# Gated linear attention and an MLP on one core: 32x32 transposes of alpha, k and q done in place, the reordering left to the readers

## The chip, the cores and the metric

The kernel runs on one core of a Trainium2 chip. The time is device microseconds of one execution; lower is better. Five engines each take their own instructions in the order in which the program issued them: TensorE (PE, with its weight loads shown apart as PEld), VectorE (DVE), ScalarE (ACT), GpSimd (POOL) and SyncE (SP, which here issues the DMAs).

## The reference

```python
# q, k, v, alpha: (4, 8, 768, 48) float32;  alpha in [0.8, 1)
state = np.zeros((B, H, D, D))
for t in range(S):
    state = alpha[:, :, t, :, None] * state + np.einsum('bhd,bhe->bhde', k[:, :, t], v[:, :, t])
    y[:, :, t] = np.einsum('bhd,bhde->bhe', q[:, :, t], state)

x = y.transpose(0, 2, 1, 3).reshape(3072, 384)     # tokens x (heads*dim)
h = x @ w_in                                        # 384 x 2048
g = h * np.clip(h + 3.0, 0.0, 6.0) / 6.0            # hardswish
out = g @ w_out                                     # 2048 x 384
```

## The kernel before

**Chunks.** The 4 x 768 tokens are cut into 24 chunks of 128 (six to a batch entry). A chunk j turns the recurrence into matrix products: with running products of alpha along the tokens, k is scaled by a decay and q by a growth, `scores` multiplies the two, `masked` cuts the upper triangle, `attend` multiplies with v and with the state of the chunk before, and `update`/`next_state` carry the state on. All this wants alpha, k and q with heads and dims on the partitions and tokens in the free direction, in four tiles of 128 x 128 (two heads each), while the inputs have tokens first.

**How the inputs are turned.** Chunks 0 to 5 are turned by TensorE through PSUM. From chunk 6 on (`FIRST`) each of alpha, k and q is loaded into a "quad" tile `quads[name, j % 2]` of 128 x (4, 4, 48), whose 32-partition groups and 32-column pieces are 32x32 blocks, and `by_blocks` (line 286) has VectorE transpose the blocks. A load spreads neighbouring tokens over the blocks: token 4u+v of a tile lies in block v at column u. So `by_blocks` writes each transposed block with a step of four elements into the tile where tokens stand in order: `aX` for alpha (step `ca`), `Ks` for k (`tk`), `Qs` for q (`tq`).

**The steps of a chunk around the change.** `la`, `lk`, `lq` load into the quads; `ca.j` places alpha; `decay` (`r.j`, line 309) is a scan over alpha on VectorE and `growth` (`p.j`, line 320) another; `scaled` multiplies k by the decay (`k.j`) and q by the growth (`q.j`), both at line 332, in place in `Ks` and `Qs`. From chunk 8 on `turn_k` (`kt.j`, line 391) transposes the scaled k by blocks back into the k quad, from which two DMAs (`kw`, `kr`) make the copy with tokens on the partitions. ScalarE's steps are copies and activations: `qa` (line 366) and `sv` (line 419) place q and the state for `attend` (`ya`, `yb`, line 455), `cy` (line 464) keeps the chunk's y.

**The MLP.** Two chunks make a group g. Both products use sums of blocks that save multiplications (combined weights and combined x and g, made by VectorE). `M.g.i` (line 600) are the 20 products of the first layer. ScalarE copies some of them out of PSUM (`n.g.i`, line 606), VectorE adds them (`o`, lines 537 to 541), ScalarE applies the Relu part of hardswish (`e`, line 494) and VectorE the rest (`h`, line 498). VectorE makes sums of g (`s`, lines 647 and 664), `P.g.i` (line 703) are the seven products of the second layer, ScalarE keeps three of them half-way (`K.g.i`, line 682) and VectorE and ScalarE make the outputs (`G`, lines 719 and 716). The weights come first: float64 bits are loaded and turned to float32 by steps `w` and `d1` to `d4` on ScalarE, VectorE and GpSimd (`d1.i` is line 186, `d4.i` line 217), while the first six chunks run, and `x` (line 647) and `y` (lines 537 to 541) make the combined weights of the second and the first layer.

**The order.** All steps are written out by hand as words in one list (`ca.16` is step `ca` of chunk 16, `K.5.2` step `K` of group 5, number 2). The program issues them in that order, and every engine works off its own instructions in that order; semaphores make an instruction wait for what it needs. For the neighbourhoods that the prediction uses, the list reads:

```
fr.0.4.0 d3.14 k.6 q.6 ca.7 fg.0.4 d1.14 d4.14 x.0 y.1
qa.15.0 ... ca.16 lv.18.2 lk.17 la.18 sv.18.0 K.5.2 e.6.1.1 n.6.18.10 K.5.1 P.5.5 G.5.2.3 r.16 k.16
n.6.13.14 o.6.4.0 ca.17 o.6.2.0 ya.15.1 ya.14.2 yb.14 sv.15.1 yb.15 cy.15
n.9.10.10 ca.22 r.22 k.22 sm.20.1 m.20 st.21 p.21 q.21 qa.20.0
```

Of the kernel before, what the change touches and what calls it, by code (L numbers as in the profile page):

```python
# [13 lines left out]
ALU = mybir.AluOpType  # L14
# [3 lines left out]
def kernel(  # L18
# [32 lines left out]
    nc = tc.nc  # L51
# [9 lines left out]
    G = 2  # L61
    GT = G * C
    HB = C // 2
    W = C + 1
# [169 lines left out]
    BLK = 32  # L234
# [39 lines left out]
    def transposed(name, j, i=None):  # L274
        if j >= FIRST:
            t = (K_t if name == "k" else Q_t)[j] = (Ks if name == "k" else Qs)[j % 2]
            by_blocks(t, name, j)
            return
        t = bank("t" + name, j, i)
        src = ring[name, j % NR]  # L280
        for p in range(NP):
            nc.tensor.transpose(  # L282
                t[:, p], src[:, 2 * p : 2 * p + 2].rearrange("s h d -> s (h d)"), ident)

    def by_blocks(to, name, j):
        nc.vector.transpose(out=to.rearrange("r p (u v) -> r p v u", v=V),
                            in_=quads[name, j % NQ][:, :, :, 0:BLK])
# [6 lines left out]
    def without_first(t):  # L294
        return t[:, 0 : NP * W].rearrange("r (p w) -> r p w", w=W)[:, :, 1:W]

    def place_alpha(j):
        to = without_first(aX[j % 2])
        if j < FIRST:
            nc.scalar.copy(out=to, in_=ps_t.pop(("ta", j)))  # L300
        else:
            by_blocks(to, "a", j)
# [21 lines left out]
    def scaled(name, j):  # L324

        if j < FIRST:
            src = ps_t.pop(("t" + name, j))
            t = (Ks if name == "k" else Qs)[j % 2]
        else:
            src = t = (K_t if name == "k" else Q_t)[j]  # L330
        by = R_t[j][:, :, 1:W] if name == "k" else without_first(P_t.pop(j))
        nc.vector.tensor_tensor(out=t, in0=src, in1=by, op=ALU.mult)  # L332
        (K_t if name == "k" else Q_t)[j] = t
# [416 lines left out]
    with tc.manual_schedule():  # L750
# [3 lines left out]
               dx.0 w.2 d2.2 kb.1.0 ck.1 lq.1 r.2 sm.0.1 st.1 tq.1.2 q.1 d3.2 z.0.3 d1.2 dx.2 lv.1.1  # L754
               u.1.3.1 sv.1.0 sm.1.0 p.2 sm.1.1 sc.1.0.2 m.1 ya.0.3 yb.0 cy.0 lq.2 w.1 d1.1 tq.2.1
               q.2 d4.2 lk.2 tk.2.3 k.2 fa.2.0 d4.0 st.2 sc.2.0.2 d2.1 d3.1 m.2 dx.1 d4.1 qa.1.1
               lk.3 la.3 ta.3.1 ca.3 la.4 fa.0.1 sv.1.1 w.3 r.3 ta.4.3 ca.4 r.4 tk.3.1 k.3 kb.2.0
               qa.1.0 d2.3 ya.1.2 yb.1 cy.1 fa.1.2 lq.3 ck.2 d1.3 p.3 d3.3 lv.2.2 u.2.3.2 sm.2.0
               d4.3 fb.2 tq.3.1 q.3 fb.1 qa.2.0 sm.2.1 sv.2.0 st.3 fr.0.2.0 fg.0.2 lk.4 tk.4.0
               sv.2.1 w.5 d2.5 k.4 d3.5 d1.5 qa.3.0 d4.5 qa.2.1 sc.3.1.3 m.3 w.6 d2.6 d1.6 d3.6 d4.6  # L760
               lv.3.0 lq.4 w.7 kb.3.2 fb.0 f.0.3.3 kb.4.0 ya.2.1 ck.3 u.3.3.2 sm.3.0 fr.0.3.1 fg.0.3
               fr.0.1.0 fg.0.1 qa.3.1 sv.3.0 sm.3.1 p.4 d2.7 sv.3.1 d1.7 d3.7 d4.7 f.0.5.0 fr.0.5.1
               fr.0.0.0 fg.0.5 fg.0.0 tq.4.3 ck.4 la.5 ta.5.2 f.0.6.3 ca.5 w.4 d2.4 ya.3.0 yb.3 cy.3
               fr.0.6.1 yb.2 cy.2 w.9 d2.9 q.4 qa.4.1 d1.4 d1.9 dx.4 la.6 w.8 d3.4 r.5 lk.5 w.10
               d3.9 p.5 ca.6 fg.0.6 d4.9 w.12 lq.5 lv.4.1 d2.8 d3.8 f.0.7.2 d1.8 st.4 d4.8 d4.4 w.11
               fr.0.7.0 fg.0.7 f.1.7.0 fr.1.7.1 fg.1.7 sc.4.0.2 m.4 f.1.1.1 fr.1.1.0 fg.1.1 f.1.3.3
               fr.1.3.1 d2.10 d1.10 tk.5.3 f.1.0.2 d2.12 d3.10 d4.10 w.13 fg.1.3 fr.1.0.0 fg.1.0 k.5
               d3.12 lq.6 f.1.6.0 f.1.2.1 u.4.1.0 sm.4.0 d1.12 d4.12 sv.4.0 qa.4.0 ya.4.2 fr.1.6.1
               fg.1.6 w.15 tq.5.3 fa.4.3 sv.4.1 d2.11 kb.5.1 d2.13 fr.1.2.0 f.1.4.2 fr.1.4.1 d1.11
               sm.4.1 q.5 r.6 d3.11 d3.13 fg.1.4 d4.11 lv.5.0 lk.6 tq.6 p.6 d2.15 d3.15 fg.1.2 d1.13  # L770
               d4.13 sc.5.0.3 yb.4 f.1.5.0 fr.1.5.1 fg.1.5 tk.6 m.5 b.1.0.2 fb.4 b.1.1 d1.15 d4.15
               st.5 y.5 w.14 la.7 lk.7 cy.4 d2.14 qa.5.1 ck.5 b.0.0.1 fr.0.4.0 d3.14 k.6 q.6 ca.7
               fg.0.4 d1.14 d4.14 x.0 y.1 y.10 b.0.1 y.0 y.2 u.5.2 P.1.0.0 K.1.0 qa.5.0 sv.5.0
               qa.6.1 P.1.1.3 b.0.2 b.1.2 kb.6.0 ya.5.3 y.6 s.1.0.0 sm.5.0 sv.5.1 G.1.0.0 tk.7
               s.1.1.1 s.1.2.3 x.1 yb.5 cy.5 b.1.3 sc.6.1.2 lv.6.2 ck.6 u.6.3.0 s.1.3.2 x.2 P.1.2
               b.0.3 K.1.1 y.7 s.1.4 s.1.5 y.11 y.3 r.7 xc.2.1 x.3 y.4 y.8 xc.2.3 k.7 xc.2.0 xc.2.4
               y.9 y.12 y.16 y.13 y.15 P.1.3.3 K.1.2 P.1.4 bo.1 P.1.5 xc.2.5 G.1.1.1 P.1.6 y.14 y.17
               y.19 xc.2.6 sm.6.0 G.1.2.2 y.20 M.2.0.2 lv.12.1 la.8 O.1.1 O.1.0 ca.8 y.18 y.21 y.23
               so.1 G.1.3.3 n.2.0.8 bo.0 lq.7 lv.7.0 O.1.2 m.6 xc.2.2 xc.2.10 xc.2.7 tq.7 r.8 p.7
               xc.2.8 sv.6.1 M.2.15.3 M.2.1 kb.7.3 n.2.1.9 M.2.16 M.2.2 n.2.2.10 M.2.7.0 n.2.7.11  # L780
               sm.6.1 xc.2.9 q.7 p.8 M.2.3 M.2.4 n.2.4.12 M.2.8 o.2.0.0 M.2.5 n.2.5.13 qa.7.0 sv.6.0
               st.7 lk.8 O.1.3 lq.8 lk.9 la.9 la.10 tk.8 tq.8 lq.10 lq.9 ya.6.1 yb.6 M.2.9 z.1.3
               M.2.18.1 o.2.1.0 e.2.1.1 M.2.10 cy.6 ck.7 sc.7.0.2 u.7.1.3 n.2.10.14 M.2.11 qa.7.1
               ca.9 la.11 y.22 M.2.6.2 h.2.1 q.8 m.7 e.2.0.0 h.2.0 n.2.11.15 qa.6.0 n.2.18.10 qa.8.1
               M.2.12 M.2.19 n.2.12.12 M.2.13 sm.7.0 sv.7.1 r.9 k.8 o.2.3.0 sv.7.0 ya.7.0 y.24
               o.2.5.0 n.2.13.12 o.2.2.0 yb.7 cy.7 sc.8.1.2 xc.3.1 o.2.2.1 e.2.2.1 xc.3.3 o.2.3.1
               M.2.14 xc.3.4 xc.3.0 xc.3.5 o.2.4.0 xc.3.7 xc.3.6 o.2.6.0 P.2.0.1 M.3.0.2 M.2.17
               h.2.2 o.2.6.1 e.2.3.0 h.2.3 o.2.7.0 K.2.0 n.3.0.12 M.3.1 n.3.1.9 e.2.5.1 M.3.7.0
               n.3.7.13 xc.3.8 o.2.7.1 xc.3.2 kt.8 e.2.6.0 h.2.6 tk.9 M.3.2 n.3.2.10 e.2.4.0 P.2.1.3
               h.2.4 h.2.5 s.2.0.14 e.2.7.0 G.2.0.1 h.2.7 M.3.3 M.3.4 n.3.4.8 k.9 s.2.1.11 M.3.8  # L790
               o.3.0.0 ca.10 kt.9 P.2.3.3 s.2.2.15 s.2.3.14 lv.8.2 kw.8 kr.8 lk.10 sm.7.1 xc.3.9
               M.3.5 n.3.5.11 K.2.2 e.3.0.1 xc.3.10 M.3.9 o.3.1.0 P.2.2 K.2.1 u.8.0.3 M.3.18.2 s.2.5
               M.3.10 n.3.10.14 n.3.18.15 e.3.1.0 s.2.4 P.2.4 tq.9 h.3.0 st.8 sv.8.0 M.3.11 n.3.11.8
               tk.10 p.9 sm.8.0 q.9 r.10 k.10 qa.9.0 qa.9.1 m.8 sm.8.1 h.3.1 M.3.19 o.3.5.0 kt.10
               P.2.5 G.2.2.0 st.9 M.3.12 sc.9.0.1 qa.8.0 n.3.12.10 o.3.3.0 kw.9 lv.9.0 kr.9 sv.8.1
               u.9.2.3 sm.9.0 sv.9.1 sv.9.0 G.2.1.2 sm.9.1 st.10 M.3.15.2 M.3.16 M.3.6.3 M.3.13 m.9
               o.3.4.0 o.3.6.0 tq.10 n.3.13.10 o.3.2.0 e.3.4.1 ya.8.2 yb.8 ya.9.3 yb.9 cy.9 M.3.14
               M.3.17 cy.8 xc.4.1 P.2.6 e.3.5.0 G.2.3.3 o.3.2.1 xc.4.3 h.3.4 xc.4.4 o.3.6.1 xc.4.5
               xc.4.0 xc.4.6 e.3.2.1 M.4.0.0 n.4.0.10 P.3.0.1 xc.4.7 o.3.7.0 p.10 h.3.5 o.3.3.1
               xc.4.8 M.4.7.3 M.4.1 xc.4.2 h.3.2 o.3.7.1 lk.11 O.2.2 tk.11 e.3.6.0 e.3.3.1 h.3.3  # L800
               P.3.1.2 e.3.7.1 n.4.1.13 M.4.2 K.3.0 ca.11 q.10 h.3.6 r.11 k.11 h.3.7 n.4.7.15
               lv.10.2 lv.11.0 kw.10 sc.10.0.1 kr.10 G.3.0.0 u.10.3.2 sm.10.0 qa.10.1 n.4.2.14 M.4.3
               M.4.4 M.4.8 s.3.0.9 xc.4.9 s.3.2.12 s.3.1.11 P.3.3.2 n.4.4.8 M.4.5 o.4.0.0 e.4.0.0
               sv.10.1 sm.10.1 xc.4.10 kt.11 O.2.0 O.2.3 lq.11 m.10 s.3.3.9 s.3.5 M.4.9 o.4.1.0
               P.3.2 sv.10.0 st.11 n.4.5.11 K.3.2 la.13 M.4.18.0 p.11 tq.11 lk.12 tk.12 K.3.1 M.4.10
               n.4.10.9 q.11 qa.10.0 n.4.18.12 e.4.1.1 la.12 s.3.4 ca.12 h.4.0 r.12 P.3.5 G.3.2.1
               h.4.1 M.4.11 P.3.4 n.4.11.8 M.4.12 n.4.12.14 qa.11.0 M.4.19 p.12 G.3.1.3 lq.12 kw.11
               O.2.1 tq.12 kr.11 u.11.3 sc.11.0.2 sv.11.0 O.3.1 lk.13 P.3.6 qa.11.1 M.4.6.2 G.3.3.2
               k.12 o.4.3.0 m.11 sm.11.0 sv.11.1 kt.12 M.4.13 n.4.13.14 q.12 o.4.3.1 e.4.3.0 o.4.2.0
# [6 lines left out]
               lq.13 O.3.0 O.3.3 lv.13.2 kw.13 O.4.0 lq.14 tq.13 lq.15 M.5.3 M.5.4 M.5.8 s.4.3.10  # L816
# [116 lines left out]
```

## Time and profile before

| what | value |
|---|---|
| median of 3 runs | 535.56 us (535.33 to 535.83) |
| span of the profiled execution, first to last instruction | 533.7 us |
| busy: PE, PEld, DVE, ACT, POOL | 524.6, 499.4, 477.2, 257.2, 50.4 us |
| line 286 transposes (54) | 20.1 + 20.1 + 20.2 us |
| line 332 products of chunks 6 on (36) | 12.2 + 13.6 us |
| granted TensorE clock | 1.000 |

The profile is one execution, and its own time is the span; what lies around the span (about 1.9 us against the median of the timed runs) has no instruction of the program in it. In the views, "line engine operation out<-in xcount | busy, mean ns of one | idle before" is a group of instructions; a timeline row gives the start in us from the beginning of the span, the time taken, and the idle time before it with what ended it. Neighbouring instructions of an engine overlap a little, so that a duration is some tens of nanoseconds more than the distance to the next start. A view does not print the words of the order: they were matched to the rows by counting each engine's instructions in the order of the list.

### The profile page before, as it was taken

Reading aid. Unit: us, or ns where it says so; the run is one execution under the profiler, and the core shown is the slowest. Engines: PE = TensorE matmul, PEld = TensorE weight load, DVE = VectorE, ACT = ScalarE, POOL = GpSimd, SP = SyncE. Lnnn points to the kernel's source line nnn. Section 1 sums busy time; section 2 is a strip of 40 time slices with the busy share of each in tenths; the row PEclk is TensorE's granted clock in tenths of the full one; section 3 lists DMA queues with packets and bytes.
Section 4 is the critical chain, followed back from the end, with each engine's and each line's share of the span. In section 5 each row is a group of like instructions: output and inputs, shape, how many; then the busy total and the mean of one; then the engine's idle time right before and its main releaser. Section 6 shows DMA issues by size and latency. Waiting matters only on the chain.

```text
span 533.7 us, 15143 instructions
## 1 busy us (share of the span) xinstructions
PE 524.6 (98%) x6306; PEld 499.4 (94%) x6306; DVE 477.2 (89%) x849; ACT 257.2 (48%) x503; POOL 50.4 (9%) x71
## 2 busy tenths in 40 slices
PE   8799999999999999999999999999999999999997
PEld 7698886789999999999999999999999999999997
DVE  6999989999999999998999999999999899496382
ACT  3889865212653553553544444642634544553340
POOL 5333425100000000000000000000000000000000
DMA  9998876005615155254344355044454042100001
GB/s 174 217 252 256 215 216 152 21 2 154 152 30 116 32 121 135 57 140 95 87 110 113 91 124 140 19 120 102 115 136 104 11 110 43 44 2 2 15 16 37
DMA packets 124100, 54.40 MB, mean 102 GB/s; under 512 B 83328, under 2 KB 116864, under 8 KB 124032
## 3 DMA queue, kind: packets, MB, share of 16 engines
q1 hardware_dynamic: 124032, 53.44, 42.5%
q8 instruction: 49, 0.80, 0.6%
q14 instruction: 19, 0.16, 0.1%
HBM read 44.50 MB, written 8.91 MB: 100 GB/s over the span
## 4 chain that ended last, share of the span: by engine, by line
PE 85%; DVE 8%; POOL 2%; DMA 2%; ACT 1%; issue 1%; SPq 1%; DVEq 0%; POOLq 0%
PE m_ps L703 34%; PE m_ps L600 34%; PE m_ps L478 5%; PE t_ps L455 4%; PE t_ps L346 2%; PE t_ps L429 2%; PE m_ps L489 2%; PE t_ps L282 1%; DVE rings L647 1%; DMA v<-in_v_dram 1%; DVE raw L537 1%; ACT raw L191 1%; DMA kq<-in_k_dram 1%; DVE g_sb L647 1%; DVE w L537 1%
## 5 line engine op out<-in xcount | busy, mean ns | idle before, releaser
L606 ACT COPY g_sb<-m_ps 128x512 f32<-128x512 f32 x110 | 63.6, 584 | 124.9 <-PE m_ps L600 104.1
L703 PE MATMUL m_ps<-w,g_sb 128*128 128x192 f32 x704 | 121.7, 327 | 0.0
L703 PEld LDWEIGHTS m_ps<-w,g_sb 128*128 128x128 f32 x704 | 113.7, 190 | 0.4
L703 PE MATMUL m_ps<-rings,g_sb 128*128 128x192 f32 x528 | 91.5, 326 | 0.0
L703 PEld LDWEIGHTS m_ps<-rings,g_sb 128*128 128x128 f32 x528 | 85.4, 190 | 0.1
L600 PE MATMUL m_ps<-xc,w 128*128 128x128 f32 x640 | 82.7, 277 | 0.3 <-DVE w L541 0.3
L600 PEld LDWEIGHTS m_ps<-xc,w 128*128 128x128 f32 x640 | 77.5, 192 | 1.5 <-issue 0.5
L494 ACT ACTIVATE r<-g_sb,half 128x512 f32<-128x512 f32 x80 | 56.8, 722 | 32.9 <-DVE g_sb L541 12.1
L498 DVE SCALAR_TENSOR_TENSOR g_sb<-r,g_sb 128x512 f32<-128x512 f32 x80 | 53.6, 682 | 4.6 <-ACT r L494 4.2
L600 PE MATMUL m_ps<-xT,raw 128*128 128x128 f32 x400 | 52.5, 277 | 0.0
L600 PEld LDWEIGHTS m_ps<-xT,raw 128*128 128x128 f32 x400 | 48.6, 192 | 0.6
L409 POOL TENSOR_TENSOR st<-sm,R 128x192 f32<-128x192 f32 x20 | 12.9, 643 | 353.8 <-DVE sm L439 306.7
L647 DVE TENSOR_TENSOR g_sb<-g_sb 128x512 f32<-128x512 f32 (+1 forms) x55 | 42.0, 795 | 0.2
L600 PE MATMUL m_ps<-xT,w 128*128 128x128 f32 x320 | 42.0, 276 | 0.0
L600 PEld LDWEIGHTS m_ps<-xT,w 128*128 128x128 f32 x320 | 39.3, 192 | 0.1
L366 ACT COPY A<-q 48x256 f32<-48x256 f32 x88 | 35.5, 404 | 5.0 <-DVE q L332 3.7
L356 DVE TENSOR_TENSOR A<-t_ps,mask 64x256 f32<-64x256 f32 x96 | 36.0, 414 | 0.4
L478 PE MATMUL m_ps<-xT,w 128*128 128x256 f32 x144 | 32.8, 382 | 0.0
L600 PE MATMUL m_ps<-xc,raw 128*128 128x128 f32 x240 | 31.8, 276 | 0.0
L309 DVE TENSOR_TENSOR_SCAN R<-t,ones 128x516 f32<-128x516 f32 x24 | 29.7, 1236 | 1.1 <-ACT t L300 1.0
L478 PEld LDWEIGHTS m_ps<-xT,w 128*128 128x128 f32 x144 | 26.7, 190 | 3.6
L600 PEld LDWEIGHTS m_ps<-xc,raw 128*128 128x128 f32 x240 | 29.6, 192 | 0.1
(104 smaller groups left out, 731.0 us busy)
## 6 DMA issues: line engine op xcount, KB each, us to landing
raw<-in_moe_w_out_dram SPq DMA_DIRECT2D x8, 768.0 KB, 5.2
raw<-in_moe_w_in_dram SPq DMA_DIRECT2D x6, 768.0 KB, 6.8
v<-in_v_dram SPq DMA_DIRECT2D x48, 96.0 KB, 3.0
out_dram<-oh SPq DMA_DIRECT2D x44, 96.0 KB, 1.7
far<-kq SPq DMA_DIRECT2D x64, 64.0 KB, 2.2
kb<-far SPq DMA_DIRECT2D x64, 64.0 KB, 2.0
aq<-in_alpha_dram SPq DMA_DIRECT2D x36, 96.0 KB, 2.5
qq<-in_q_dram SPq DMA_DIRECT2D x36, 96.0 KB, 2.4
```

The source lines that it names most:

```text
L309: nc.vector.tensor_tensor_scan(out=reverse(R, n - 1, n), data0=reverse(ax, n, n), data1=reverse(ones, n, n), initial=0.0, op0=ALU.mult, op ...
L356: nc.vector.tensor_tensor(out=to[:, a], in0=sc[a][half], in1=mask[half, half].unsqueeze(1).to_broadcast([HB, NP, HB]), op=ALU.mult)
L366: nc.scalar.copy(out=to[:, a], in_=Q_t[j][64 * a : 64 * a + D, :, half])
L409: nc.gpsimd.tensor_tensor(out=st, in0=sm, in1=R_t[j][:, :, 0:1].to_broadcast([C, NP, D]), op=ALU.mult)
L455: nc.tensor.matmul(y_of(j, (i + 1) // 2, p)[:, HB * b : HB * b + HB], vb[:, p, e : e + 32], A_t[j][:, b, 2 * p + a], start=(b == 0 and i = ...
L478: nc.tensor.matmul(h[:, f], w1[:, kk, o : o + C], xT_t[g][:, kk], start=(kk == 0), stop=(kk == KT - 1))
L494: nc.scalar.activation(out=to, in_=h, func=AF.Relu, bias=half, scale=1.0 / 6.0)
L498: nc.vector.scalar_tensor_tensor(out=to, in0=r, scalar=1.0, in1=h, op0=ALU.min, op1=ALU.mult)
L600: nc.tensor.matmul(acc[g][i][:, f * C : (f + 1) * C], spots[w][:, f * C : (f + 1) * C], x_of(g, x), start=(first and f == 0), stop=last, s ...
L606: nc.scalar.copy(out=slots[z], in_=acc[g][i])
L647: nc.vector.tensor_tensor(out=out, in0=in0, in1=in1, op=ALU.subtract)
L703: nc.tensor.matmul(to[g], a, rhs[:, f], start=(first and f == 0), stop=(last and f == HF - 1), skip_group_check=True)
```

## The change

For chunks 6 on, `by_blocks` transposes each block onto itself, with runs of 32 neighbouring elements on both sides. Nothing is reordered there. `scaled` reads its first operand from the quad in permuted order: consecutive elements lie 48 elements (192 bytes) apart, four of them, and then the next token by one element; its second operand and its output are contiguous. For alpha a new instruction on ScalarE (`nc.scalar.copy`, in step `ca.j` right after the transpose) reads the quad in that permuted order and writes `aX` in order. The quad of q is thereby read until `q.j` rather than until `tq.j`, and five loads of q (`lq.10`, `lq.15`, `lq.18`, `lq.21`, `lq.22`) stand later in the list, each behind the `q` step of two chunks before. No other word moves.

```diff
     def transposed(name, j, i=None):
         if j >= FIRST:
-            t = (K_t if name == "k" else Q_t)[j] = (Ks if name == "k" else Qs)[j % 2]
-            by_blocks(t, name, j)
+            by_blocks(name, j)
             return
...
-    def by_blocks(to, name, j):
-        nc.vector.transpose(out=to.rearrange("r p (u v) -> r p v u", v=V),
-                            in_=quads[name, j % NQ][:, :, :, 0:BLK])
+    def blocks(name, j):
+        return quads[name, j % NQ][:, :, :, 0:BLK]
+
+    def by_blocks(name, j):
+        nc.vector.transpose(out=blocks(name, j), in_=blocks(name, j))
+
+    def by_fours(t):
+        return t.rearrange("r p (u v) -> r p u v", v=V)
+
+    def in_order(name, j):
+        return blocks(name, j).rearrange("r p v u -> r p u v")
...
     def place_alpha(j):
...
         else:
-            by_blocks(to, "a", j)
+            by_blocks("a", j)
+            nc.scalar.copy(out=by_fours(to), in_=in_order("a", j))
...
     def scaled(name, j):
+        t = (Ks if name == "k" else Qs)[j % 2]
+        by = R_t[j][:, :, 1:W] if name == "k" else without_first(P_t.pop(j))
         if j < FIRST:
-            src = ps_t.pop(("t" + name, j))
-            t = (Ks if name == "k" else Qs)[j % 2]
+            nc.vector.tensor_tensor(out=t, in0=ps_t.pop(("t" + name, j)), in1=by, op=ALU.mult)
         else:
-            src = t = (K_t if name == "k" else Q_t)[j]
-        by = R_t[j][:, :, 1:W] if name == "k" else without_first(P_t.pop(j))
-        nc.vector.tensor_tensor(out=t, in0=src, in1=by, op=ALU.mult)
+            nc.vector.tensor_tensor(out=by_fours(t), in0=in_order(name, j), in1=by_fours(by),
+                                    op=ALU.mult)
         (K_t if name == "k" else Q_t)[j] = t
```

## The prediction

> **What bounds the kernel now.** I read the page's busy times and slices first, then busy time by stretches, then the groups by shape, then the timeline around each `ca` step.
>
> ```profile
> span 533.7 us, 15143 instructions
> ...
> PE 524.6 (98%) x6306; PEld 499.4 (94%) x6306; DVE 477.2 (89%) x849; ACT 257.2 (48%) x503; POOL 50.4 (9%) x71
> ...
> PE   8799999999999999999999999999999999999997
> ...
> DVE  6999989999999999998999999999999899496382
> ```
>
> ```profile
> 128.00:440.00 312.00, 311.96 (x4042) 306.64 (x4043) 298.67 (x551) 147.71 (x309) 10.63 (x16) 1.00 0.43 100
> ```
>
> From 128 to 440 us PE shows 311.96 of 312 us busy at clock 1.00, and its weight loads 306.64. So PE is the bound; freeing another engine can return at most the 5.4 us in which no weight load ran. DVE is busy 298.67, idle 13.3: it runs right behind PE and often delivers just in time. ACT is half idle. So the change has little to win, and what counts is whom it makes wait.
>
> ```profile
> L286 DVE STREAM_TRANSPOSE t<-aq 128x512 f32<-128x512 f32 x18 | 20.1, 1115 | 0.0
> L332 DVE TENSOR_TENSOR q<-q,P 128x512 f32<-128x512 f32 x18 | 13.6, 754 | 0.1
> L332 DVE TENSOR_TENSOR k<-k,R 128x512 f32<-128x512 f32 x18 | 12.2, 676 | 0.0
> L391 DVE STREAM_TRANSPOSE kq<-k 128x512 f32<-128x512 f32 x16 | 11.2, 697 | 0.0
> L191 ACT ACTIVATE raw<-raw 128x768 f16<-128x768 int32 x3 | 5.8, 1941 | 0.1
> L606 ACT COPY g_sb<-m_ps 128x512 f32<-128x512 f32 x110 | 63.6, 584 | 124.9 <-PE m_ps L600 104.1 <-DVE g_sb L647 9.7 <-DVE g_sb L498 5.7
> ```
>
> **Transposes.** Line 286 writes with a step of 16 bytes, 1.12 us; line 391 has the same size and runs on both sides, 0.70 us. In place all runs are contiguous: 3 x 0.42 = 1.26 us less DVE time per chunk, 18 chunks.
>
> **Products.** No row reads with a large step on DVE. Below, 0.68 us as now; above, twice that, 1.36. If a scattered read costs what the scattered write cost, 0.68 + 0.42 = 1.10. I take 1.2, between the last two: +0.52 for each. DVE per chunk is then -1.26 + 1.04 = -0.22 us, 4 us in all (ends: -22.7 and +1.8 us over the run).
>
> [...]
>
> **The copy on ACT.** 0.58 us as the contiguous copy of line 606; above, line 191's 1941 ns for 768 scattered elements, 1.29 us for 512. I take 0.58 + 0.42 = 1.0. As work, 18 us on a half-idle engine cost nothing. As a place in ACT's queue it costs: the copy cannot start before DVE's transpose, all of ACT's later steps stand behind it, and DVE works later than the list suggests. Hence I went through all 18 places: copy start = the later of the transpose's end less 0.42 and the end of ACT's step before; the following steps shift by what is left; a consumer is late by what exceeds its slack. Chunk 16 is the clearest (ACT, DVE, PE):
>
> ```profile
> 291.49 0.32 ACT L682 COPY p<-m_ps 128x192 f32<-128x192 f32 x1
> 291.84 0.72 ACT L494 ACTIVATE r<-g_sb,half 128x512 f32<-128x512 f32 x1
> ...
> 294.59 1.12 DVE L286 STREAM_TRANSPOSE t<-aq 128x512 f32<-128x512 f32 x1
> 296.50 0.36 DVE L719 TENSOR_TENSOR oh<-m_ps,u 128x192 f32<-128x192 f32 x1 [0.79 <-issue]
> ...
> 293.64 2.77 PE L703 MATMUL m_ps<-w,g_sb 128*128 128x192 f32 x16
> ```
>
> `ca.16` stands ahead of `K.5.2` (the line 682 row) in the list. Now ACT starts `K.5.2` at 291.49, three microseconds before DVE gets to the transpose. After, ACT stands still until then. DVE last waited for PE at 268.9; since then it ran three of the transposes (-1.26) and three products (+1.56): +0.30. Transpose end 295.71 + 0.30 - 0.42 = 295.59, copy to 296.59, `K.5.2` to 296.95 with a hand-over. `P.5.5` (PE, 293.64) writes on into the bank that `K.5.2` copies: **3.3 us** of standing PE. The rest of that queue (`n.6.18.10`, `n.6.10.15`) is late by less.
>
> Chunk 17: `sv.15.1` starts at 306.34, `ca.17`'s transpose ends at 308.46, and `yb.15` on PE already waits for `sv.15.1`. DVE itself slips about 2.2 us behind chunk 16's jam (`G.5.2.3` waits for `K.5.1`, then k.16 +0.52, one transpose -0.42): transpose end 308.46 + 2.2 - 0.42 = 310.2, copy to 311.25, `sv.15.1` to 312.0 where it ended at 307.07: 4.9, of which 3.3 is counted: **1.6 us**.
>
> Chunk 22: `ca.22` and `r.22` are neighbours, and the copy has to follow `n.9.10.10`.
>
> ```profile
> 415.38 0.59 ACT L606 COPY g_sb<-m_ps 128x512 f32<-128x512 f32 x1 [4.22 <-PE m_ps L600]
> ...
> 413.04 1.10 DVE L286 STREAM_TRANSPOSE t<-aq 128x512 f32<-128x512 f32 x1
> 414.17 1.23 DVE L309 TENSOR_TENSOR_SCAN R<-t,ones 128x516 f32<-128x516 f32 x1
> ```
>
> The copy runs 415.97 to 416.97, the scan starts at 417.05 instead of 414.17: 2.9 us of standing DVE, and `k.22`, `sm.20.1`, `m.20` queue behind it. With `k.22`'s +0.52, `m.20` ends 3.4 us later; it ended 0.85 us before `ya.20`: **2.5 us**.
>
> Chunk 9: DVE is early, but ACT is busy to 142.10 and its next copies (`n.2.11`, `n.2.12`) end 0.11 us before PE continues in their banks. 1.0 us of copy plus the 0.2 that the row of steps loses: **1.2 us**. Chunk 19: ACT stands from 338.8 to about 342, `n.7.12.11` reaches `M.7.13` late by 0.5 to 1.1: **0.8**. Chunk 18: `e.6.5.1` 1.2 late, `h.6.5`, `h.6.7` behind it with 0.62 us of slack before `P.6.3`: **0.5**. Chunk 11: `n.4.2.14` 0.82 late against 0.39: **0.4**.
>
> Chunk 7, in the weights stage, where DVE is busy 47.59 of 48 us (80 to 128) and PE waits for its last weight sum (0.29 us at 128.04): the copy now stands ahead of `d1.14` (ACT, 90.15 to 91.08), which `d4.14` (POOL) and then `x.0` (DVE, 96.43) need. Two transposes (-0.84), k.6 (+0.52) and q.6 come before; q.6 took 1.95 because POOL's `d4.14` ran beside it, which moves away: 1.2, -0.75. Transpose end 95.79 - 1.07 - 0.42 = 94.3; copy to 95.35, `d1.14` 0.93, `d4.14` 1.46 (the undisturbed row at 86.03): `x.0` at 97.85, +1.4. Two transposes and one product up to 128: -0.3. **1.1 us**.
>
> Chunks 6, 8, 10, 12 to 15, 20, 21, 23: the delayed steps (up to 2.2 us) have more slack than that on the way to PE; chunk 6's 1.2 us on DVE ends in the 1.28 us wait before `sm.4.0`. If that cover were gone, each would cost PE its 0.5 to 2 us.
>
> **Loads.** The same DMAs in number and size. The five moved `lq` pass `la.11` and a few words of SP's queue and wait for a `q` step; they land about 2.4 us after issue and are wanted tens of microseconds later. `la` now waits for ACT's copy rather than the transpose, by one to two microseconds, ahead of loads wanted later: nothing.
>
> **Sum.** 3.3 + 1.6 + 2.5 + 1.2 + 0.8 + 0.5 + 0.4 + 1.1 = 11.4 us. Against it, a late PE gives DVE a lead, and DVE is 0.22 us a chunk shorter, so part of the 5.4 us of loading gaps closes; I take 1.4. +10.0 us on the span: 543.7; the median lies 1.9 above the span: **545.6 us**.
>
> **Rivals.**
> *Blocks absorbed.* With products at 0.68 and the copy at 0.58, DVE reaches each transpose up to 1.3 us earlier: chunk 16 gives 1.35, 17 1.0, 22 1.6, 9 0.7, 7 nothing, 4.6 together, less up to 3 closed gaps: +1.6 to +4, 537 to 539.5. For it: the contiguous rows; against: line 286's price for scattered access. 0.14.
> *Faster.* The same prices, and each lead of 1.26 us per chunk lasts to the next `ca`, so that ACT never stands: PE gets back half of its 5.4 us: 532.9. It decides only if DVE's waits behind PE (1.19 us at 187, 1.35 at 247) do not eat the lead; they do. 0.08.
> *DVE becomes the bound.* The in-place transposes stay at 1.12 (the 48-element pitch sets it, not the write), so the change does not do what it says, or the reads cost 2 us: +1.0 to +1.4 per chunk, 17 to 25 us on DVE against 13.3 idle, and each jam grows by about 1 us: +17 to +25, 553 to 561. 0.12.
> *No difference.* Delays and recovered gaps cancel. 0.04.
>
> **Numbers.** The forecast (slower by 4 to 17 us) has 0.62. Two tenths of a per cent, 1.07 us, is what a measurement of this kernel can tell. Slower 0.62 + 0.14 + 0.12 = 0.88, same 0.04, faster 0.08. For 8 in 10 the range runs from the absorbed case's lower end, 537, to 556, inside the DVE-bound case.
>
> **What would show it.** Line 286 near 0.70 us; line 332 of chunks 6 on near 1.2 us; a new ACT copy near 1.0 us, waiting for line 286 some 20 us in total; PE waits in front of `P.5.5`, `yb.15`, `ya.20` and near 143 us; DVE waiting for ACT before line 309. Wrong: PE as full as now from 128 to 440, or DVE with no idle time left there.

## The result and the profile after

The changed kernel takes 551.43 us (median of 4 runs, 551.35 to 553.21) against 535.69 before on the same chip: a ratio of 1.0302, 95% interval 1.0287 to 1.0316. It is 15.7 us slower; the forecast was +10, with a range that reaches to 556. The span of the profiled execution grew from 533.7 to 549.6 us, by 15.9. (The run of 553.21 us had a mean granted clock of 0.991, the other three 0.994; what the clock does is shown below.)

The page of the changed kernel, the same rows as before:

```profile
span 549.6 us, 15194 instructions
...
PE 530.2 (96%) x6306; PEld 502.6 (91%) x6306; DVE 469.8 (85%) x849; ACT 274.9 (50%) x521; POOL 50.3 (9%) x71
...
PE   7799999999999999999997899899999899999997
...
DVE  6999898899999899998896878799989799497282
```

VectorE has 7.4 us less work than before (477.2), ScalarE 17.7 us more, and neither is busier than 85%. What is new are the slices of PE that are no longer full, in the second half of the run. The stretch from 128 to 440 us shows the same:

```profile
128.00:440.00 312.00, 302.36 (x3813) 295.13 (x3812) 279.53 (x522) 155.29 (x311) 10.44 (x15) 0.99 0.42 96
```

PE is busy 302.36 us of 312 (311.96 before) and VectorE 279.53 (298.67 before). No engine took over as the bound: both wait more. The clock column says 0.99, where it said 1.00; that is the second loss, shown below.

The groups by shape give the prices (line numbers moved by up to ten; 288 are the transposes, 339 the products, 310 the new copy):

```profile
L310 ACT COPY t<-aq 128x512 f32<-128x512 f32 x18 | 19.4, 1080 | 34.3 <-DVE aq L288 31.6 <-DMA kb<-far 2.7
L339 DVE TENSOR_TENSOR q<-qq,P 128x512 f32<-128x512 f32 x18 | 18.4, 1024 | 0.1
L339 DVE TENSOR_TENSOR k<-kq,R 128x512 f32<-128x512 f32 x18 | 18.3, 1019 | 0.0
L288 DVE STREAM_TRANSPOSE aq<-aq 128x512 f32<-128x512 f32 x18 | 12.6, 699 | 0.1
```

A transpose in place takes 0.70 us (1.12 before), a product 1.02 (0.68), the copy 1.08. The number to look at is behind the bar of the first row: ScalarE stood 34.3 us in front of these 18 copies, 31.6 of it waiting for the transposes of line 288. ScalarE is busy for only 50% of the run, and a wait of it need not cost anything (in a version below these copies wait 17.0 us and the time is that of the kernel before); here the steps behind it were due.

The timeline around chunk 16 (ScalarE, VectorE, TensorE):

```profile
297.29 1.05 ACT L310 COPY t<-aq 128x512 f32<-128x512 f32 x1 [3.86 <-DVE aq L288]
298.25 0.31 ACT L690 COPY p<-m_ps 128x192 f32<-128x192 f32 x1
...
296.54 0.71 DVE L288 STREAM_TRANSPOSE aq<-aq 128x512 f32<-128x512 f32 x1
303.25 0.36 DVE L727 TENSOR_TENSOR oh<-m_ps,u 128x192 f32<-128x192 f32 x1 [6.00 <-issue]
...
298.61 4.55 PE L711 MATMUL m_ps<-w,g_sb 128*128 128x192 f32 x16 [2.76 <-ACT p L690]
```

ScalarE waits 3.86 us for the transpose, copies, and only then makes `K.5.2` (line 690), for which TensorE has stood 2.76 us. And then `P.5.5`, 2.77 us before, takes 4.55. (Its sixteen rows, x16, are eight products: the trace counts each twice.) Two stretches of the windows, one at this place and one at chunk 17, with the granted clock third from the end:

```profile
298.60:303.00 4.40, 4.39 (x17) 4.39 (x18) 0.00 (x0) 3.06 (x7) 0.00 (x0) 0.61 0.74 162
...
316.20:320.30 4.10, 4.10 (x48) 3.82 (x49) 0.98 (x3) 1.21 (x4) 0.00 (x0) 0.58 0.54 118
```

After each of the two longest waits, 2.76 and 2.25 us, the clock falls, to 0.61 and 0.58 on average over these stretches: (1 - 0.61) x 4.4 + (1 - 0.58) x 4.1 = 3.4 us of TensorE's time. The other places, on the timeline, chunks 7, 17, 19 and 22 in order:

```profile
97.77 1.76 DVE L655 TENSOR_TENSOR rings<-w 128x1536 f32<-128x1536 f32 x1 [2.82 <-POOL w L217]
...
316.17 1.03 PE L463 MATMUL t_ps<-A,v 128*32 128x64 f32 x32 [2.25 <-ACT v L427]
...
355.37 0.71 ACT L427 COPY v<-s 48x192 f32<-48x192 f32 x2
355.40 1.16 PE L608 MATMUL m_ps<-xc,raw 128*128 128x128 f32 x8 [0.76 <-ACT g_sb L614]
...
356.17 0.36 DVE L447 TENSOR_TENSOR s<-t_ps,st 128x192 f32<-128x192 f32 x1 [3.13 <-issue]
...
357.78 0.94 PE L608 MATMUL m_ps<-xT,raw 128*128 128x128 f32 x6 [1.23 <-DVE g_sb L545]
...
431.19 1.23 DVE L317 TENSOR_TENSOR_SCAN R<-t,ones 128x516 f32<-128x516 f32 x1 [3.34 <-ACT t L310]
434.28 1.56 PE L463 MATMUL t_ps<-A,v 128*32 128x64 f32 x64 [1.35 <-DVE A L364]
```

The brackets name what a row waited for: `x.0` for the weight step on GpSimd, `yb.15` for ScalarE's `sv.15.1`, `M.7.13` for `n.7.12.11`, `M.7.15` for VectorE, the scan `r.22` for the copy, `ya.20` for the mask behind that scan. The bracket of the row at 356.17 (`sm.17.0`) names nothing; just before it, at 356.08, ScalarE's `sv.16.1` (the row at 355.37) ended.

### The profile page after: what moved, and what is told of

Same layout as the page of the kernel before. It is cut to its first block, busy times and chain, and to the rows that moved or that the text cites. A ratio compares the mean times of both kernels' runs of the same rounds, so it can differ in the third digit from the quotient of the medians.

```text
span 549.6 us, 15194 instructions
## 1 busy us (share of the span) xinstructions
PE 530.2 (96%) x6306; PEld 502.6 (91%) x6306; DVE 469.8 (85%) x849; ACT 274.9 (50%) x521; POOL 50.3 (9%) x71
## 5 line engine op out<-in xcount | busy, mean ns | idle before, releaser
L711 PE MATMUL m_ps<-w,g_sb 128*128 128x192 f32 x704 | 123.8, 330 | 2.8 <-ACT p L690 2.8
L711 PEld LDWEIGHTS m_ps<-w,g_sb 128*128 128x128 f32 x704 | 115.3, 192 | 3.8 <-ACT p L690 2.9
L608 PE MATMUL m_ps<-xc,w 128*128 128x128 f32 x640 | 84.4, 280 | 1.2 <-DVE w L549 0.7
L608 PEld LDWEIGHTS m_ps<-xc,w 128*128 128x128 f32 x640 | 78.8, 194 | 2.7 <-ACT g_sb L614 1.5
L608 PEld LDWEIGHTS m_ps<-xT,w 128*128 128x128 f32 x320 | 39.3, 192 | 0.1
L310 ACT COPY t<-aq 128x512 f32<-128x512 f32 x18 | 19.4, 1080 | 34.3 <-DVE aq L288 31.6
L463 PE MATMUL t_ps<-A,v 128*32 128x64 f32 x1536 | 26.5, 221 | 4.7 <-ACT v L427 2.2
```

The lines of the kernel that those rows point to most:

```text
L310: nc.scalar.copy(out=by_fours(to), in_=in_order("a", j))
L463: nc.tensor.matmul(y_of(j, (i + 1) // 2, p)[:, HB * b : HB * b + HB], vb[:, p, e : e + 32], A_t[j][:, b, 2 * p + a], start=(b == 0 and i = ...
L608: nc.tensor.matmul(acc[g][i][:, f * C : (f + 1) * C], spots[w][:, f * C : (f + 1) * C], x_of(g, x), start=(first and f == 0), stop=last, s ...
L711: nc.tensor.matmul(to[g], a, rhs[:, f], start=(first and f == 0), stop=(last and f == HF - 1), skip_group_check=True)
```

## Experiments

Two theories. **Queue:** the loss comes from the place of the alpha copy in an engine's queue, ahead of steps that are due, and from the clock that falls after the longest waits. **VectorE:** it comes from the products' permuted reads, which make VectorE late. All ratios are against the kernel before, on the same chip. Differences to the changed kernel (551.43 us) are between medians that were not all taken on one chip; the kernel before measured 535.46 to 535.69 us beside them.

**k and q alone.** Alpha goes the old way; no copy on ScalarE.

```diff
-            by_blocks("a", j)
-            nc.scalar.copy(out=by_fours(to), in_=in_order("a", j))
+            nc.vector.transpose(out=to.rearrange("r p (u v) -> r p v u", v=V),
+                                in_=blocks("a", j))
```

> Queue theory (the loss comes from the place of the alpha copy in ScalarE's queue): k and q are turned in place and their products read in permuted order, alpha goes the old way with no copy on ScalarE; VectorE saves 2 x 0.42 and pays 2 x 0.34 us a chunk, so nothing waits anew: 534.5 to 536.5 us, within 0.2% of the kernel before. VectorE theory (the loss comes from the permuted reads of the products): about 551 us, as all of them are in it.

536.06 us, ratio 1.0015 (1.0006 to 1.0025). All 36 permuted products are in it, at 1.02 and 1.09 us, and the whole version is only 0.6 us slower. The VectorE theory falls.

**Alpha alone.** k and q go the old way.

```diff
-            by_blocks(name, j)
+            t = (K_t if name == "k" else Q_t)[j] = (Ks if name == "k" else Qs)[j % 2]
+            nc.vector.transpose(out=t.rearrange("r p (u v) -> r p v u", v=V), in_=blocks(name, j))
...
-            nc.vector.tensor_tensor(out=by_fours(t), in0=in_order(name, j), in1=by_fours(by),
-                                    op=ALU.mult)
+            nc.vector.tensor_tensor(out=t, in0=t, in1=by, op=ALU.mult)
```

> Queue theory: only alpha is turned in place and put in order by ScalarE, k and q as before; all the jams of ScalarE's queue are there: 548 to 553 us, line 310 waiting some 30 us for the transposes. VectorE theory: the products are at 0.68 us again and one transpose a chunk is shorter, so VectorE has 7.5 us less to do than before: 533 to 536 us.

549.65 us, ratio 1.0272 (1.0256 to 1.0287): 14.2 of the 15.7 us with only the copy on ScalarE and one shorter transpose. The run in its profile, whose two longest waits are those of the changed kernel (2.8 and 2.3 us) and whose mean clock is 0.994 as there, took 551.23 us, as long as the changed kernel; the other three, with a mean clock of 0.997, took 549.43 to 549.85. So what is missing goes with the clock and not with the products, as far as four runs tell. The group row of the copy reads as in the changed kernel:

```profile
L311 ACT COPY t<-aq 128x512 f32<-128x512 f32 x18 | 19.4, 1080 | 32.5 <-DVE aq L289 32.4
```

**One place mended, chunk 16.** `ca.16` is split into the transpose `cb.16`, which stays, and the copy `cc.16`, four ScalarE steps later.

```diff
-ca.16 lv.18.2 lk.17 la.18 sv.18.0 K.5.2 e.6.1.1 n.6.18.10 K.5.1 P.5.5
+cb.16 lv.18.2 lk.17 sv.18.0 K.5.2 e.6.1.1 n.6.18.10 K.5.1 cc.16 la.18 P.5.5
```

> The changed kernel, with one word moved: the copy of chunk 16's alpha stands behind K.5.1 in ScalarE's queue instead of ahead of K.5.2 (the next load of alpha into that quad follows it). Queue theory: P.5.5 no longer waits 2.8 us and TensorE's clock does not fall after it (1.8 us); chunk 17's jam stays or grows a little: 545.5 to 548 us. VectorE theory: no VectorE instruction is changed, 551 to 552 us.

547.52 us, ratio 1.0233 (1.0201 to 1.0266): 3.9 us less than the changed kernel. Timeline of that kernel, ScalarE and TensorE:

```profile
293.99 0.32 ACT L696 COPY p<-m_ps 128x192 f32<-128x192 f32 x1
...
297.83 1.07 ACT L316 COPY t<-aq 128x512 f32<-128x512 f32 x1 [1.45 <-DVE aq L288]
...
296.23 2.77 PE L717 MATMUL m_ps<-w,g_sb 128*128 128x192 f32 x16
```

`K.5.2` runs almost four microseconds ahead of the copy, `P.5.5` no longer waits and takes 2.77 us, as in the kernel before at clock 1.00. The jam of chunk 17 is still there: `yb.15` waits 2.1 us.

**Keeping TensorE busy in the two longest waits.** Unneeded products fill them; the waits stay.

```diff
-P.5.5
+zt.1.12 P.5.5        # 12 x matmul(banks[1][:, 0:C], ident, ident)
...
-yb.15
+zt.0.10 yb.15        # 10 of them into banks[0]
```

> The changed kernel with 12 unneeded 128x128 products ahead of P.5.5 and 10 ahead of yb.15, into PSUM banks that are free there; the waits themselves stay. If the clock fell to one half because TensorE stood still: P.5.5's sixteen products take 2.8 us instead of 4.55 and the time is 2.5 to 3.5 us less, 548 to 549 us. If those stretches are slow for another reason (ScalarE's late n.6.18.10, VectorE): 551 to 552 us.

548.48 us, ratio 1.0248 (1.0232 to 1.0264), 2.95 us less than the changed kernel, with more instructions. Its timeline of TensorE, the filling (line 544) first:

```profile
295.62 2.84 PE L544 MATMUL t_ps<-ident 128*128 128x128 f32 x24
298.58 2.87 PE L715 MATMUL m_ps<-w,g_sb 128*128 128x192 f32 x16
```

(The trace counts each product twice, here 12 as x24, as in `P.5.5`.) `P.5.5` starts at 298.58, as late as in the changed kernel (298.61), but takes 2.87 us and not 4.55, and the clock of the run is 1.000. So these 3 us belong to the clock, and they come on top of the waits.

**The copy on GpSimd.**

```diff
-            nc.scalar.copy(out=by_fours(to), in_=in_order("a", j))
+            nc.gpsimd.tensor_copy(out=by_fours(to), in_=in_order("a", j))
```

> The changed kernel with the copy of alpha on GpSimd instead of ScalarE, at the same places in the list. Queue theory: ScalarE's queue is as before and its jams are gone; GpSimd's copy, estimated at 1.5 to 2.5 us, makes the decay scan wait where it follows closely (chunks 11, 12, 16, 22): 536 to 542 us. If any copy between transpose and scan costs the time, whatever engine makes it: 550 us or more. VectorE theory: 551 us.

540.06 us, ratio 1.0087 (1.0072 to 1.0102). The copy takes 1.25 us there; the 1.5 to 2.5 us expected were an estimate that no run shows. About half of what is left, 2.2 us, comes at one place, on the timeline of GpSimd and TensorE:

```profile
267.64 1.06 POOL L310 COPY t<-aq 128x512 f32<-128x512 f32 x1 [12.91 <-DMA v<-in_v_dram]
268.76 0.52 POOL L423 MEMSET v<- 64x512 f32 x1
...
269.34 1.55 PE L463 MATMUL t_ps<-A,v 128*32 128x64 f32 x96 [2.05 <-POOL v L423]
```

Here the copy of chunk 15 stands ahead of GpSimd's memset for `sv.12.0`, which `ya.12` needs: the same jam on another engine. (The bracket of the copy's row names a DMA of long before; its transpose had just ended.) The time is as expected, but not for the reason given: the scans of chunks 11, 12, 16 and 22 made TensorE lose next to nothing; it fell behind at chunks 7 and 15, where other steps of GpSimd stood behind the copy, and by smaller steps elsewhere.

**The same with two words moved:** the copy of chunk 7 behind `d4.14`, that of chunk 15 behind `sv.12.0`.

```diff
-ca.7 fg.0.4 d1.14 d4.14 x.0
+cb.7 fg.0.4 d1.14 d4.14 cc.7 x.0
...
-ca.15 sv.12.0
+cb.15 sv.12.0 cc.15
```

> The kernel with the copy on GpSimd, with two words moved: the copy of chunk 7 stands behind d4.14 and the copy of chunk 15 behind sv.12.0 (a memset of v on GpSimd that it held up for 2.4 us before ya.12). Queue theory: 537 to 538 us, 2.4 to 3.2 us less than with the copies ahead. If GpSimd's copies cost by their length or by sharing VectorE's way to memory: 540 us.

537.04 us, ratio 1.0025 (1.0015 to 1.0035): 3.0 us less than with the copies ahead.

**Thirteen places mended, the copy on ScalarE.** Ten copies stand a few words later; in chunks 9, 16 and 22 transpose and load stand earlier.

```diff
-ca.17 o.6.2.0 ya.15.1 ya.14.2 yb.14 sv.15.1 yb.15 cy.15 kw.16 lk.18 cy.14
+cb.17 o.6.2.0 ya.15.1 ya.14.2 yb.14 sv.15.1 yb.15 cy.15 kw.16 lk.18 cy.14 cc.17
...
-s.8.5 P.8.2 o.9.1.0 M.9.10 K.8.2 sv.20.0 n.9.10.10 ca.22 r.22
+s.8.5 cb.22 P.8.2 o.9.1.0 M.9.10 K.8.2 sv.20.0 cc.22 n.9.10.10 r.22
...
```

> The changed kernel, all computation kept, with step ca of thirteen chunks split in two words, transpose and copy: the copies of chunks 6, 7, 13 to 15, 17 to 21 stand a few words later, behind the ScalarE steps that they held up; in chunks 9, 16 and 22 the transpose (and the load of alpha) stands earlier, so that the copy falls in a gap of ScalarE. Queue theory: P.5.5, yb.15, M.7.13, M.7.15 and ya.20 no longer wait and the clock stays at 1.0: 534 to 537 us, 14 to 17 us below the changed kernel with the same instructions. VectorE or copy-work theories: 548 us or more, as no instruction is taken away.

535.72 us, ratio 1.0004 (0.9995 to 1.0013): the whole loss is gone with the same arithmetic, the same permuted reads and the same 18 copies. Its windows row from 128 to 440 us and its group row of the copy:

```profile
128.00:440.00 312.00, 311.91 (x4039) 306.27 (x4039) 293.03 (x549) 162.68 (x324) 10.15 (x16) 1.00 0.42 98
```

```profile
L316 ACT COPY t<-aq 128x512 f32<-128x512 f32 x18 | 19.5, 1085 | 17.0 <-DVE aq L288 14.2 <-DMA kb<-far 2.7
```

PE is as full as before (311.91; 311.96). The copies still wait 17.0 us, now where nothing behind them is due. VectorE's 293.03 is 5.6 us less than before, and this bought nothing.

**Only four of them:** chunks 16, 17, 19, 22.

> The changed kernel with only four of the thirteen places mended, those of chunks 16, 17, 19 and 22, as in the kernel where all thirteen are. Queue theory, by the places where TensorE fell behind in the changed kernel (12.9 us at these four with the clock's share, 1.65 at chunks 7 and 9, the rest small): 537 to 539 us. If the loss is spread over all eighteen copies: 546 us or more (14/18 of 15.7 us left).

539.03 us, ratio 1.0064 (1.0046 to 1.0082), at the upper end of what was expected: mending four places of eighteen takes away 12.4 of the 15.7 us. What is left at chunks 7 and 9 (1.65 us) and elsewhere is a little more than the differences there add up to.

No version was faster than the kernel before.

## Why the prediction was right, step by step

**The bound** was read right: PE was full, VectorE right behind it, ScalarE half idle; less work on VectorE (the mended kernel) returned nothing.

**The prices.** Transposes: 0.70 as said. The copy 1.08, said 1.0. The products were over-estimated, 1.02 and not 1.2: the scattered read costs 0.34 us, less than the scattered write (0.42), so the value lies below the two ends between which I chose (1.10 and 1.36; the upper, twice 0.68, was my estimate, and no run shows it). Here scattered reads had a price as line 286's scattered write had: the product went from 0.68 to 1.02 us, ScalarE's copy took 1.08 against 0.58 for a contiguous one from PSUM. Had reads cost nothing, VectorE would have been shorter by 22.7 us; it became shorter by 7.4. The copies' wait for the transposes was under-estimated: 31.6 us in total, where some 20 were said.

**The places.** With the first instruction of every word matched in both traces, TensorE falls behind like this (us; the last column is where it was seen):

| chunk | said | measured | at |
|---|---|---|---|
| 7 | 1.1 | 1.0 | `M.2.0`, `M.2.1` |
| 9 | 1.2 | 0.65 | `M.2.12` |
| 11 | 0.4 | 0 | |
| 16 | 3.3 | 3.1 | `P.5.5` |
| 16, clock | not seen | 1.8 | `P.5.5` to `M.6.19` |
| 17 | 1.6 | 2.4 | `yb.15` |
| 17, clock | not seen | 1.7 | `M.6.6` to `P.5.6` |
| 18 | 0.5 | 0 | |
| 19 | 0.8 | 2.4 | `M.7.13`, `M.7.15` |
| 21 | 0 | 0.7 | `M.8.17`, `P.8.0` |
| 22 | 2.5 | 1.9 | `ya.20`, `yb.20` |
| closed gaps | -1.4 | 0 | |

With 0.25 at `M.3.5` the measured column adds up to 15.9, the growth of the span. Chunk 7's `x.0` was said to start at 97.85 and started at 97.77; `q.6`, which took 1.95 us beside GpSimd's `d4.14` (the median of its row was 0.68), took 1.02 with that step moved to 96.27.

**What was mis-sized.** The sum of 10.0 was short by 5.9. (1) It had no term for the clock: 3.5 by this table, 2.95 by the run that filled the waits. The trace of before did not show it: PE's longest wait there, after its first product, is 0.95 us. (2) The 1.4 us taken off for closed gaps did not come. (3) In chunk 19, I followed ScalarE's late steps to TensorE alone. `sv.16.1` reads the state that `sm.17.0` overwrites, so VectorE waited 3.13 us, and `o.7.5.0` behind it gave `M.7.15`'s bank free too late: 1.5 us. (4) At chunk 16, `G.5.2.3` does not wait for `K.5.1` alone, as I wrote, but for the result of `P.5.5` itself; VectorE slipped by as much as TensorE, and chunk 17's jam kept its full size, 2.4 instead of 1.6. (5) Chunks 11 and 18 cost nothing, 9 and 22 less than said: about 2 us together. (6) Chunk 21 and `M.3.5`, 0.95 us together, were put at nothing. That (3), (5) and (6) go the way that this table says is read from the traces; no run took them one by one. So the mechanism and its main places were right, and the misses went both ways; that 551.43 us lies within the range is owed to its width (537 to 556), as the sum found less than two thirds of the loss.

**The rivals.** VectorE as the bound is ruled out by the kernel with k and q alone; blocks absorbed, the faster case and no difference by the result; and the change did what it says (a transpose at 0.70 us, not 1.12).

## What to carry to other kernels

On this kernel an instruction in a queue that is worked off in order cost what stood behind it while it waited, not its own length (18 copies of 1.08 us: 551.43 us with due steps behind them, 535.72 with thirteen places mended). So for every instruction that is put on a half-idle engine, compare when its input is really ready in the trace (not in the list) with when the next step of that engine starts now, and follow the late steps to every reader, also those that wait for a buffer to be free. Split the producer from the reader in the order, and put the reader behind the steps that are due, or the producer earlier. And on this kernel, bound by one full engine, work taken off another one (5.6 us of VectorE's, in the version with thirteen places mended) returned nothing.

## What the runs showed of the hardware

**TensorE's clock after a wait.** In the changed kernel, after TensorE's first product, the granted clock stayed at 1.00 through waits of up to 1.35 us and fell to 0.50 for 3.41 us after the waits of 2.76 and 2.25 us: 1.8 and 1.7 us lost. In the kernel with the copy on GpSimd a wait of 2.05 us left the clock of the profiled run at 1.000. The kernel with one place mended, whose longest wait is 2.1 us in its profile, had a mean clock of 0.994 in three of four runs and of 1.000 in the fourth. Early in its profiled run there are two shorter waits, and the 64 products behind them took 1.93 us; in the changed kernel, behind the dots, the same 64 took 1.10 us at clock 1.00 after waits of 0.96 and 0.83 us:

```profile
19.95 0.74 PE L443 MATMUL t_ps<-v,kb 64*64 64x48 f32 x29 [0.95 <-issue]
22.06 1.93 PE L469 MATMUL t_ps<-A,v 128*32 128x64 f32 x64 [0.84 <-DVE s L453]
...
22.19 1.10 PE L463 MATMUL t_ps<-A,v 128*32 128x64 f32 x64 [0.83 <-DVE s L447]
```

So the length alone does not decide.

These are the stretches before, during and after the first fall of the changed kernel, and before, during and after its second (TensorE's busy time is the number behind the first comma, the clock the third from the end):

```profile
295.97:299.38 3.41, 0.77 (x5) 0.77 (x6) 1.25 (x3) 2.09 (x4) 0.00 (x0) 1.00 0.36 89
299.38:302.79 3.41, 3.41 (x12) 3.41 (x12) 0.00 (x0) 2.28 (x6) 0.00 (x0) 0.50 0.84 183
302.79:316.44 13.65, 11.40 (x242) 10.84 (x241) 12.01 (x22) 5.47 (x12) 1.03 (x2) 1.00 0.21 40
313.03:316.44 3.41, 1.16 (x81) 1.00 (x69) 2.31 (x4) 1.66 (x4) 0.00 (x0) 1.00 0.51 81
316.44:319.85 3.41, 3.41 (x40) 3.13 (x29) 0.53 (x2) 0.91 (x3) 0.00 (x0) 0.50 0.56 130
319.86:549.60 229.74, 223.52 (x2493) 219.33 (x2492) 180.23 (x334) 100.20 (x200) 3.66 (x6) 1.00 0.27 63
```

Each fall lasts 3.41 us, and 13.65 us, four times as much, lie between the two. In the 3.41 us before them TensorE was busy for 0.77 and 1.16 us; with unneeded products in both waits the clock of the profiled run was 1.000. What sets the length of a fall, and how much work in which stretch keeps the clock up, was not tried.

**Scattered access.** Elements 192 bytes apart cost VectorE 0.34 us more for 512 of them as one of two operands (0.68 to 1.02), ScalarE 0.50 us (0.58 to 1.08, from SBUF against a contiguous copy from PSUM), and a write with a step of 16 bytes 0.42 us (0.70 to 1.12).
